# phi's positive part moved from GpSimd to ScalarE, with a new order of all steps, in an fp32 attention and two-MLP kernel on one core

## The chip, the cores and the metric

The kernel runs on one core of a Trainium2 chip. A core has a matrix engine (TensorE, in the profile PE, with PEld for its weight loads), VectorE (DVE), ScalarE (ACT), GpSimd (POOL) and SyncE (SP), which here only issues DMAs. Each engine takes its instructions strictly in the order in which the program lists them and waits on semaphores for the others. The metric is the device time of one execution in microseconds (us), as the median of several runs.

## The reference

The input is a batch of 4 with 8 heads, 576 tokens and 64 columns per head, all in fp32. Attention mixes a causal softmax with a memory read through a feature map phi; two MLPs over the 2304 tokens follow.

```python
def phi(x): return np.where(x > 0, x, np.exp(x) - 1.0) + 1.0
local = softmax(causal(q @ k.T / sqrt(D))) @ v
mem   = (phi(q) @ M_prev) / (phi(q) @ z_prev + 1e-6)
x = g * mem + (1 - g) * local                 # g = sigmoid(beta), one per head
h = x @ w_in;  x = (h * tanh(softplus(h))) @ w_out      # 512 -> 2048 -> 512
h = x @ w_in2; out = (h * sigmoid(h)) @ w_out2
```

phi(x) equals exp(min(x, 0)) + max(x, 0), which is the form that the kernel computes.

## The kernel before, in words

**Attention** runs first, in 16 pairs of heads (`pair_steps` lists the steps of one pair, with an engine, an estimated duration and the steps that they depend on; `Attn.steps` holds the instruction of each). For a pair, PE makes the scores in blocks of 128 queries (`s4`, `s3`, `s2`, `s1`, `s0`, L582 and L621). DVE reads each block from PSUM, adds the mask and takes the row maximum (`r..`, L575). ACT makes the exponentials with their row sums (`e..`, L602). PE transposes the probabilities (`X1`, `X2`, `X3`, `W`, L483), DVE and ACT copy them out of PSUM (L476, L473), and PE multiplies by v and the memory matrix (`Vhi`, `Vlo`, L679). DVE scales the result into `xT` (L683).

**phi** is a side chain of each pair on tile `nq` (128 x 576): `phn` = min(q, 0), `phe` = its exponential on ACT (L503), `phu` = max(q, 0), `phf` = their sum (L505), all but `phe` on POOL. Then POOL multiplies by z_prev (`phz` L506, `phy` L509), DVE adds up and inverts (`phr` L510, `phg` L511, `phd` L513, `phq` L514), and POOL scales phi by the result into the tiles that PE transposes together with the probabilities (`phmh`, `phml` L528, `phm0` L533). POOL also spreads the softmax's divisors (`zg` L631, `n00` L634), which DVE makes (`za` L628, `zd` L630). Tiles `e` and `u` have two buffers each.

**The MLPs** follow on the same core, each product split into seven fp32r products of halves (L985 to L987 for the first matrix, L1053 for the second). Their weights are decoded on ACT and DVE (L789, L799, L801, L803, L806) and the first ones also combined on POOL (L832, L851, L854); eight of these weight tiles are decoded while attention runs or just after it. The first input operands are split by ACT and DVE (L956, L949) from `xT`.

**The order.** `Steps.plan` builds one order of all steps of the whole program before any instruction is issued: at each moment it gives each free engine, out of the steps whose inputs and buffers are there by the estimated durations, the one with the earliest due time. The due times are moved by a table, `SHIFT`, one number for each kind of step. So durations in `pair_steps` and the numbers in `SHIFT` decide where each instruction stands in each engine's queue, attention and MLPs alike. `gate` steps turn beta into g: a load on SP, an exponential on ACT (L431) and ten small operations on DVE (L434 to L449).

Of the kernel before, what the change touches and what calls it, by code (L numbers as in the profile page):

```python
# [202 lines left out]
P = 128  # L203
# [3 lines left out]
ST = 64  # L207
# [9 lines left out]
def mm(n, k=1):  # L217
    return k * max(0.109, n / 2215)
# [40 lines left out]
def pair_steps():  # L259
# [4 lines left out]
    E("phn", "G", 0.75, ["ldnq"])  # L264
    E("phe", "A", 0.58, ["phn"])
    E("phu", "G", 0.75, ["ldnq"])
    E("phf", "G", 1.25, ["phe", "phu"])
    E("phz", "G", 1.25, ["phf"])
    E("phy", "G", 0.36, ["phf"])
# [8 lines left out]
    for i in (4, 3, 2, 1):  # L278
        for x in range(2 if i == 4 else 1):
            n = SA if i == 4 else width(i)  # L280
            E(f"s4{x}" if i == 4 else f"s{i}", "P", mm(n, 4) + 0.07, qk)
# [14 lines left out]
        if i == 1:  # L296
            m.group("s", ("s0", "P", 0.25, qk), [("r00", "D", dve(ST), ["s0"], 0.17)])
            E("e00", "A", act(ST, False, 2), ["r00"])
            m.uses.append(("sm", "r00", ["r00"], ["e00"]))
            exps = ["e00"] + [f"e{x}{y}" for x in range(1, 5) for y in range(2)]  # L300
            E("za", "D", 0.15, exps)
            E("zd", "D", 0.15, ["za"], 0.1)
            E("zg", "G", 1.0, ["zd"])
            E("phq", "D", 0.12, ["za", "phd"])
            E("phmh", "G", 0.75, ["phq"])
            E("phml", "G", 0.75, ["phq"])
            E("phm0", "G", 0.36, ["phd"])
            E("n00", "G", 0.43, ["zd"])
            evict("W", 0.52, ["phmh", "phml"] + exps[1:], 512)
            m.twin("t", ("RT", "P", 0.30, ["zg"]), [[("RTAh", "A", act(256), ["RT"])], [("RTBh", "A", act(256), ["RT"])]])  # L310
# [5 lines left out]
        if i == 2:  # L316
            hi = [f"e{x}{j}" for x in (3, 4) for j in range(2)]
            evict("X1", 0.52, hi, 512)
            evict("X2", 0.42, hi, 384)
            V("hi", (1, 2))  # L320
        if i == 1:
            lo = [f"e{x}{j}" for x in (1, 2) for j in range(2)]
            evict("X3", 0.48, lo + ["n00", "phm0"], 384, 0.14)
            V("lo", (3,))
# [12 lines left out]
class Attn:  # L337
# [153 lines left out]
    def steps(self, p):  # L491
# [10 lines left out]
        f["phn"] = lambda: nc.gpsimd.tensor_scalar(self.get(p, "e"), s["nq"], 0.0, None, op0=ALU.min)  # L502
        f["phe"] = lambda: nc.scalar.activation(s["e"], s["e"], AF.Exp)  # L503
        f["phu"] = lambda: nc.gpsimd.tensor_scalar(self.get(p, "u"), s["nq"], 0.0, None, op0=ALU.max)
# [406 lines left out]
class Moe:  # L911
# [522 lines left out]
```

## Time and profile before

| | us |
|---|---|
| median of 3 runs (lowest, highest) | 965.44 (965.17, 966.11) |
| the profiled execution | 967.41 |
| its span, first to last instruction | 965.5 |
| attention, from the start to the first matmul of the MLPs | 195.28 |
| from there to the end | 770.2 |

The profiled execution took 1.9 us more than its span, and 2.0 us more than the median of the other runs. Lines "Lnnn" are lines of the kernel above. A group of instructions is written as line, engine, operation, output tile <- input tiles, and its busy time. The granted clock is a share of TensorE's full clock.

### The profile page before, as it was taken

How to read it: one execution, taken by the hardware profiler on the slowest of the kernel's cores; microseconds unless marked ns; L12 is line 12 of the kernel's file. 1: busy time of each engine (PE TensorE's matmuls, PEld its weight loads, DVE VectorE, ACT ScalarE, POOL GpSimd, SP SyncE). 2: the span in 40 equal slices, each digit the busy share in tenths (PEclk: the TensorE clock that was granted, in tenths of full speed). 3: DMA queues.
4: the chain of work that ended last, by engine and by line, in shares of the span. 5: the costliest groups of instructions: out<-in, count | busy, mean ns of one | idle time of the engine just before them, and what ended most of it. 6: DMA issues, size and time to landing. Idle time of an engine off the chain costs nothing.

```text
span 965.5 us, 17322 instructions
## 1 busy us (share of the span) xinstructions
PE 932.6 (97%) x6656; PEld 821.3 (85%) x6656; DVE 673.1 (70%) x1541; ACT 496.3 (51%) x1167; POOL 171.1 (18%) x191
## 2 busy tenths in 40 slices
PE   6998989889999999999999999999999999999998
PEld 4665656679999999999999999999898998989986
DVE  6898889896577668773858798947656756654333
ACT  5787888875655334442533564654533433434330
POOL 7989999600000000000000000000000000000000
PEclk9898999999999999999999999999999999999999
DMA  6443542256536811660176435623650275023512
GB/s 217 123 161 109 167 163 89 73 212 264 229 107 207 275 66 54 218 224 23 51 249 214 190 158 178 249 92 94 207 219 1 71 264 183 1 78 128 183 55 98
DMA packets 57218, 143.47 MB, mean 149 GB/s; under 512 B 6960, under 2 KB 24368, under 8 KB 57136
## 3 DMA queue, kind: packets, MB, share of 16 engines
q1 hardware_dynamic: 56992, 142.04, 42.8%
q8 instruction: 52, 0.85, 0.4%
q10 hardware_dynamic: 144, 0.33, 0.1%
q14 instruction: 30, 0.25, 0.1%
HBM read 104.60 MB, written 37.75 MB: 147 GB/s over the span
## 4 chain that ended last, share of the span: by engine, by line
PE 82%; POOL 6%; ACT 5%; DVE 4%; issue 1%; DMA 1%; SPq 0%; POOLq 0%; ACTq 0%
PE acc L1053 42%; PE psX L985 7%; PE psX L986 7%; PE psX L987 7%; PE psY L986 3%; PE psY L987 3%; PE psY L985 3%; PE ps_t L679 2%; PE psW L987 2%; PE psW L986 2%; PE psW L985 2%; PE ps_s L582 2%; PE ps_t L483 1%; POOL e L502 1%; ACT Ph L602 1%
## 5 line engine op out<-in xcount | busy, mean ns | idle before, releaser
L1053 PE MATMUL acc<-g,w 128*128 128x320 f32 (+1 forms) x1152 | 218.1, 337 | 0.0
L1053 PE MATMUL acc<-w,g 128*128 128x512 f32 x864 | 215.3, 394 | 0.0
L1053 PEld LDWEIGHTS acc<-g,w 128*128 128x128 f32 x1152 | 184.0, 188 | 13.3
L1053 PEld LDWEIGHTS acc<-w,g 128*128 128x128 f32 x864 | 157.5, 188 | 30.1
L1016 ACT COPY vt<-psX 128x256 f32<-128x256 f32 (+1 forms) x192 | 75.4, 397 | 134.3 <-PE psX L987 122.8
L1074 DVE TENSOR_TENSOR xT<-acc,xT 128x512 f32<-128x512 f32 (+1 forms) x126 | 77.2, 613 | 84.4 <-PE acc L1053 83.7
L1026 DVE TENSOR_TENSOR g<-vt,g 128x512 fp32r<-128x512 f32 (+1 forms) x128 | 94.9, 754 | 40.3 <-ACT g L1025 39.4
L1014 DVE TENSOR_TENSOR vt<-psY,vt 128x256 f32<-128x256 f32 (+1 forms) x128 | 58.0, 457 | 92.6 <-ACT vt L1016 46.1
L1025 ACT CAST g<-vt 128x512 fp32r<-128x512 f32 (+1 forms) x128 | 83.5, 672 | 36.8 <-PE acc L1053 35.7
L985 PE MATMUL psX<-x,w 128*128 128x320 f32 (+1 forms) x256 | 75.8, 296 | 0.0
L986 PE MATMUL psX<-x,w 128*128 128x320 f32 (+1 forms) x256 | 75.7, 296 | 0.0
L987 PE MATMUL psX<-x,w 128*128 128x320 f32 (+1 forms) x256 | 75.6, 295 | 0.0
L582 PE MATMUL ps_s<-kT,qT 64*128 64x288 f32 (+3 forms) x320 | 69.2, 487 | 6.2 <-DMA kT<-in_kT_dram 4.7
L1022 ACT ACTIVATE vt<-vt 128x640 f32<-128x640 f32 (+1 forms) x64 | 43.7, 685 | 47.2 <-DVE vt L1014 46.9
L1020 ACT ACTIVATE vt<-vt 128x256 f32<-128x256 f32 (+1 forms) x64 | 28.3, 444 | 74.8 <-DVE vt L1014 74.8
L575 DVE CUSTOM_DVE_ANT_0 sm<-ps_s,mask 128x320 f32<-128x320 f32 (+3 forms) x128 | 56.6, 472 | 8.9 <-PE ps_s L582 7.2
L1021 ACT ACTIVATE vt<-psX 128x256 f32<-128x256 f32 (+1 forms) x64 | 26.0, 407 | 50.2 <-PE psX L987 50.1
L1014 DVE TENSOR_TENSOR vt<-psW,vt 128x256 f32<-128x256 f32 (+1 forms) x64 | 29.1, 455 | 31.1 <-PE psW L987 29.2
L985 PEld LDWEIGHTS psX<-x,w 128*128 128x128 f32 x256 | 48.2, 188 | 1.8 <-issue 0.2
L986 PEld LDWEIGHTS psX<-x,w 128*128 128x128 f32 x256 | 48.3, 189 | 1.6
L602 ACT ACTIVATE Ph<-sm,m 128x576 f32<-128x576 f32 (+1 forms) x64 | 45.7, 720 | 6.1 <-DVE m L575 5.8
L987 PEld LDWEIGHTS psX<-x,w 128*128 128x128 f32 x256 | 48.2, 188 | 0.0
(125 smaller groups left out, 2067.6 us busy)
## 6 DMA issues: line engine op xcount, KB each, us to landing
stg<-in_moe_w_in_dram SPq DMA_DIRECT2D x32, 512.0 KB, 5.0
stg<-in_moe_w_out_dram SPq DMA_DIRECT2D x32, 512.0 KB, 4.0
x<-sp SPq DMA_DIRECT2D x18, 640.0 KB, 5.2
x<-sp SPq DMA_DIRECT2D x18, 512.0 KB, 4.0
sp<-x SPq DMA_DIRECT2D x12, 640.0 KB, 3.1
sp<-x SPq DMA_DIRECT2D x12, 512.0 KB, 4.1
nv<-in_v_dram SPq DMA_DIRECT2D x16, 320.0 KB, 3.0
x1T<-sp01T SPq DMA_DIRECT2D x8, 640.0 KB, 4.4
```

Of the source, the lines that this page charges most:

```text
L575: nc.vector.tensor_tensor_reduce(out, ps, mask, -0.125, init, ALU.add, ALU.min, acc)
L582: nc.tensor.matmul(ps, lhsT=s["qT"][R[j], qcols(i)], rhs=s["kT"][R[j], k0 + cols.start:k0 + cols.stop], start=True, stop=True)
L602: nc.scalar.activation(ptile(i)[:, o:o + w] if i else G("P0")[:, 2], s[f"sm{i}{j}"], AF.Exp, bias=s[f"m{i}"][:, j:j + 1], scale=-1.0, accu ...
L985: nc.tensor.matmul(o, lhsT=W(0, kc), rhs=X(0, kc), start=(n in (1, 2, 7) and kc == 0), stop=False, skip_group_check=True)
L986: nc.tensor.matmul(o, lhsT=W(0, kc), rhs=X(1, kc), start=False, stop=False, skip_group_check=True)
L987: nc.tensor.matmul(o, lhsT=W(1, kc), rhs=X(0, kc), start=False, stop=(kc == 1), skip_group_check=True)
L1014: nc.vector.tensor_tensor(o, self.bank[q, to], o, op=ALU.add)
L1016: f[f"s{n}"] = lambda n=n: nc.scalar.copy(val(*at[n]), self.bank[q, "X"])
L1025: f[f"h{c}"] = lambda c=c: nc.scalar.copy(hi(c), val(c))
L1026: f[f"l{c}"] = lambda c=c: nc.vector.tensor_tensor(self.gt(q, c)[:, 1, :2 * tb], val(c), hi(c).bitcast(F32), op=ALU.subtract)
L1053: nc.tensor.matmul(y, lhsT=a, rhs=b, start=(c == 0 and k == 0), stop=(c == 1 and k == 5))
L1074: nc.vector.tensor_tensor(part, acc, part, op=ALU.add)
```

## The change

max(q, 0) is now a Relu activation on ACT (`phu`), and min(q, 0) is made on POOL as q minus that (`phn`, a TENSOR_TENSOR instead of a TENSOR_SCALAR). So `phn` depends on `phu`, where before both depended on the load alone. Estimated durations of some fifteen steps are altered, and all of `SHIFT`.

```diff
-    E("phn", "G", 0.75, ["ldnq"])
+    E("phu", "A", 0.58, ["ldnq"])
+    E("phn", "G", 1.37, ["phu"])
     E("phe", "A", 0.58, ["phn"])
-    E("phu", "G", 0.75, ["ldnq"])
-    E("phf", "G", 1.25, ["phe", "phu"])
+    E("phf", "G", 1.37, ["phe", "phu"])
     E("phz", "G", 1.25, ["phf"])
-    E("phy", "G", 0.36, ["phf"])
+    E("phy", "G", 0.29, ["phf"])
...
-            E("za", "D", 0.15, exps)
+            E("za", "D", 0.1, exps)
...
-            E("phmh", "G", 0.75, ["phq"])
-            E("phml", "G", 0.75, ["phq"])
-            E("phm0", "G", 0.36, ["phd"])
+            E("phmh", "G", 0.58, ["phq"])
+            E("phml", "G", 0.58, ["phq"])
+            E("phm0", "G", 0.26, ["phd"])
...
-        f["phn"] = lambda: nc.gpsimd.tensor_scalar(self.get(p, "e"), s["nq"], 0.0, None, op0=ALU.min)
+        f["phn"] = lambda: nc.gpsimd.tensor_tensor(self.get(p, "e"), s["nq"], s["u"], op=ALU.subtract)
         f["phe"] = lambda: nc.scalar.activation(s["e"], s["e"], AF.Exp)
-        f["phu"] = lambda: nc.gpsimd.tensor_scalar(self.get(p, "u"), s["nq"], 0.0, None, op0=ALU.max)
+        f["phu"] = lambda: nc.scalar.activation(self.get(p, "u"), s["nq"], AF.Relu)
...
-    ('a', 'ldkT'): -4.8, ('a', 'ldqT'): -0.1, ('a', 'ldnq'): 2.62, ('a', 'ldnv'): 720.14, ('a', 'phn'): -463.56,
+    ('a', 'ldkT'): -8.04, ('a', 'ldqT'): 1.13, ('a', 'ldnq'): 1.53, ('a', 'ldnv'): 829.25, ('a', 'phu'): 231.88,
```

The order shows at three places what moved. First POOL in steady attention, about one pair long; `P_..` is the tile that `phm0` and `n00` write. Before:

```order
L502 TENSOR_SCALAR e<-nq 128x576
L504 TENSOR_SCALAR u<-nq 128x576 x2
L533 TENSOR_TENSOR P_278<-e,c 128x64
L505 TENSOR_TENSOR e<-e,u 128x576
L506 TENSOR_TENSOR u<-e,z 128x512
L509 TENSOR_TENSOR u<-e,y 128x64
L634 TENSOR_SCALAR P_278<-P_278,r,g1s 128x2x64
L631 TENSOR_TENSOR rx<-r,g_102 128x512
L528 TENSOR_TENSOR Pl<-e,c 128x2x128
L528 TENSOR_TENSOR Ph<-e,c 128x2x128
```

And POOL in the changed kernel, about one pair long:

```order
L502 TENSOR_TENSOR e<-nq,u 128x576
L509 TENSOR_TENSOR u<-e,y 128x64
L505 TENSOR_TENSOR e<-e,u 128x576
L506 TENSOR_TENSOR u<-e,z 128x512
L533 TENSOR_TENSOR P_424<-e,c 128x64
L509 TENSOR_TENSOR u<-e,y 128x64
L528 TENSOR_TENSOR Pl<-e,c 128x2x128
L634 TENSOR_SCALAR P_424<-P_424,r,g1s 128x2x64
L631 TENSOR_TENSOR rx<-r,g_102 128x512
L528 TENSOR_TENSOR Ph<-e,c 128x2x128
```

The L504 rows are gone; where one of them often stood between L502 and L505 of a pair there is now a short row or none.

Second the start, on DVE; `ISA` with `sm` is a score reduction of r.., and `bt` and `g` are the gate's tiles. Before:

```order
L405 MEMSET warm 128x1
L575 ISA sm,m_135<-ps_s,mask 128x288
...
L575 ISA sm,m_159<-ps_s,smask 128x64
L575 ISA m_159 128x1
L434 TENSOR_SCALAR bt_100<-bt_100 128x8
L435 RECIPROCAL g<-bt_100 128x8
```

And DVE at the start of the changed kernel:

```order
L405 MEMSET warm 128x1
L434 TENSOR_SCALAR bt_100<-bt_100 128x8
...
L449 COPY bt_105<-bt_100 64x4 x2
L575 ISA sm,m_152<-ps_s,mask 128x288
L575 ISA m_152 128x1
```

The whole gate chain now stands ahead of the first five reductions (four of 288 columns and one of 64), which stood ahead of it. On SP, the first q loads changed places too. Before:

```order
L458 DMA qT<-in_qT_dram 128x576
L458 DMA nq<-in_q_dram 128x576
L462 DMA z<-in_z_prev_dram 128x512
L467 DMA y<-in_z_prev_dram 64x4x64 x2
L428 DMA bt_100<-in_beta_dram 128x8
```

And SP's first rows in the changed kernel:

```order
L458 DMA nq<-in_q_dram 128x576
L462 DMA z<-in_z_prev_dram 128x512
L467 DMA y<-in_z_prev_dram 64x4x64 x2
L458 DMA qT<-in_qT_dram 128x576
L428 DMA bt_100<-in_beta_dram 128x8
```

qT, which the first score needs, went from first place to behind the loads of nq, z and y; beta kept its place.

Third DVE where attention ends and the first splits of the MLPs' input (L949) begin; `val` and `stg` belong to a weight tile's decoding. Before:

```order
L803 SCALAR_TENSOR_TENSOR val<-stg,val 128x512
L791 TENSOR_SCALAR val<-stg 128x512
L806 SCALAR_TENSOR_TENSOR val<-stg,val 128x512
L949 TENSOR_TENSOR x_3523<-xT,x_3523 128x512
L949 TENSOR_TENSOR x_3525<-xT,x_3525 128x512
L949 TENSOR_TENSOR xT<-xT 128x2x256
L683 TENSOR_TENSOR xT<-ps_t,R 128x256
L949 TENSOR_TENSOR xT<-xT 128x2x256
```

And DVE in the changed kernel, a few rows behind its first split:

```order
L949 TENSOR_TENSOR xT<-xT 128x2x256
L799 TENSOR_SCALAR val<-val 128x512
L683 TENSOR_TENSOR xT<-ps_t,R 128x256
L949 TENSOR_TENSOR x0T_3453<-xT,x0T_3453 128x512
L949 TENSOR_TENSOR xT<-xT 128x2x256
L801 TENSOR_SCALAR val<-val 128x512
L949 TENSOR_TENSOR x_3602<-xT,x_3602 128x640
L949 TENSOR_TENSOR x_3601<-xT,x_3601 128x640
```

Two of the first eight weight tiles (four rows each: L799, L801, L803, L806) stand behind the first split in the changed kernel; before, all eight stood ahead of it. On PE the last pair's `Vhi` now stands behind the first three products of the MLPs, where before all of attention stood ahead of them.

## Rows read from the trace of the kernel before

**Rows 1.** The page's first part: busy us, share of the span, instructions.
```profile
PE 932.6 (97%) x6656; PEld 821.3 (85%) x6656; DVE 673.1 (70%) x1541; ACT 496.3 (51%) x1167; POOL 171.1 (18%) x191
```

**Rows 2.** Windows, by stage: length; busy us of each engine; granted clock; DMA.
```profile
0.00:20.00 20.00, 11.61 (x72) 8.64 (x72) 12.58 (x48) 9.85 (x29) 14.29 (x21) 1.00 0.59 202
...
20.00:181.30 161.30, 145.93 (x1711) 98.48 (x1710) 143.65 (x509) 134.38 (x416) 150.87 (x164) 0.94 0.41 131
...
195.28:215.00 19.72, 16.18 (x115) 14.84 (x114) 18.51 (x31) 14.78 (x30) 0.98 (x1) 1.00 0.62 245
215.00:940.00 725.00, 725.00 (x4503) 673.64 (x4502) 478.12 (x912) 324.24 (x661) 0.00 (x0) 1.00 0.44 151
```

**Rows 3.** Waits of PE and DVE from 20 to 200 us: total, times, longest.
```profile
PE ps_t L483 <- POOL Pl L528: 2.3, 3, 1.4
PE ps_t L483 <- POOL Ph L528: 1.9, 3, 1.0
...
DVE c L510 <- POOL u L509: 4.2, 5, 1.2
```

**Rows 4.** One of these waits in the timeline: start, length, engine, operation.
```profile
138.05 0.34 PE L483 MATMUL ps_t<-ident,Pl 64*128 64x64 f32 x4 [1.41 <-POOL Pl L528]
```

**Rows 5.** Windows of 5 us round the last fall of the clock.
```profile
135.00:140.00 5.00, 2.91 (x44) 1.87 (x40) 4.64 (x13) 3.06 (x12) 5.00 (x8) 1.00 0.72 251
140.00:145.00 5.00, 3.94 (x42) 2.58 (x42) 3.74 (x16) 3.08 (x9) 4.20 (x4) 0.58 0.35 107
```

**Rows 6.** Groups of POOL: operation, count, busy us, mean ns, idle before and releaser.
```profile
L502 POOL TENSOR_SCALAR e<-nq 128x576 f32<-128x576 f32 x16 | 26.7, 1671 | 2.5 <-DMA nq<-in_q_dram 2.2
L504 POOL TENSOR_SCALAR u<-nq 128x576 f32<-128x576 f32 x16 | 26.4, 1650 | 0.0
L505 POOL TENSOR_TENSOR e<-e,u 128x576 f32<-128x576 f32 x16 | 23.1, 1446 | 5.1 <-ACT e L503 4.1 <-DVE c L513 0.8
```

**Rows 7.** Group of ACT: the exponential of phi.
```profile
L503 ACT ACTIVATE e<-e 128x576 f32<-128x576 f32 x16 | 11.1, 691 | 3.6 <-POOL e L502 3.5
```

**Rows 8.** Groups of three small DVE operations, to 180 us.
```profile
L628 DVE TENSOR_SCALAR z<-z 128x9 f32<-128x9 f32 x15 | 8.5, 564 | 1.7 <-ACT Pl L602 1.7
...
L514 DVE TENSOR_TENSOR c<-c,z 128x8 f32<-128x8 f32 x15 | 7.0, 468 | 0.2
L511 DVE SCALAR_TENSOR_TENSOR c<-c,bt 128x9 f32<-128x9 f32 x15 | 6.9, 457 | 0.0
```

**Rows 9.** The source line of L628: ns least, median, most.
```profile
L628 DVE TENSOR_SCALAR z<-z x16: 161/318/1402, 19.4 to 184.7; 128x9 f32<-128x9 f32 x16
```

**Rows 10.** Timeline at two places: a pass of POOL, the DVE operation beside it.
```profile
154.33 1.42 POOL L505 TENSOR_TENSOR e<-e,u 128x576 f32<-128x576 f32 x1
...
154.38 1.40 DVE L628 TENSOR_SCALAR z<-z 128x9 f32<-128x9 f32 x1
...
168.02 1.64 POOL L504 TENSOR_SCALAR u<-nq 128x576 f32<-128x576 f32 x1
...
168.23 0.47 DVE L514 TENSOR_TENSOR c<-c,z 128x8 f32<-128x8 f32 x1
```

**Rows 11.** Timeline of the start: SP's queue and DVE.
```profile
2.11 1.40 SPq L467 DMA_DIRECT2D y<-in_z_prev_dram  x2
...
6.16 0.46 DVE L575 CUSTOM_DVE_ANT_0 sm<-ps_s,mask 128x288 f32<-128x288 f32 x1 [5.31 <-PE ps_s L582]
...
7.88 0.22 DVE L575 CUSTOM_DVE_ANT_0 sm<-ps_s,smask 128x64 f32<-128x64 f32 x1
...
9.03 0.17 DVE L434 TENSOR_SCALAR bt<-bt 128x8 f32<-128x8 f32 x1 [0.93 <-ACT bt L431]
...
13.44 0.62 DVE L575 CUSTOM_DVE_ANT_0 sm<-ps_s,mask 128x448 f32<-128x448 f32 x1
```

**Rows 12.** Timeline: two of the four DVE operations of one weight tile.
```profile
190.54 0.41 DVE L801 TENSOR_SCALAR val<-val 128x512 uint32<-128x512 uint32 x1
...
192.07 0.68 DVE L803 SCALAR_TENSOR_TENSOR val<-stg,val 128x512 uint32<-128x512 uint32 x1
```

More of the change, by code (lines that the diff above doesn't have):

```diff
@@ L280, in pair_steps @@
             n = SA if i == 4 else width(i)
-            E(f"s4{x}" if i == 4 else f"s{i}", "P", mm(n, 4) + 0.07, qk)
+            E(f"s4{x}" if i == 4 else f"s{i}", "P", mm(n, 4), qk)
         for j in range(2):
@@ L296, in pair_steps @@
         if i == 1:
-            m.group("s", ("s0", "P", 0.25, qk), [("r00", "D", dve(ST), ["s0"], 0.17)])
+            m.group("s", ("s0", "P", 0.17, qk), [("r00", "D", dve(ST), ["s0"], 0.17)])
             E("e00", "A", act(ST, False, 2), ["r00"])
@@ L304, in pair_steps @@
             E("phq", "D", 0.12, ["za", "phd"])
-            E("phmh", "G", 0.75, ["phq"])
-            E("phml", "G", 0.75, ["phq"])
-            E("phm0", "G", 0.36, ["phd"])
+            E("phmh", "G", 0.58, ["phq"])
+            E("phml", "G", 0.58, ["phq"])
+            E("phm0", "G", 0.26, ["phd"])
             E("n00", "G", 0.43, ["zd"])
-            evict("W", 0.52, ["phmh", "phml"] + exps[1:], 512)
-            m.twin("t", ("RT", "P", 0.30, ["zg"]), [[("RTAh", "A", act(256), ["RT"])], [("RTBh", "A", act(256), ["RT"])]])
+            evict("W", 0.49, ["phmh", "phml"] + exps[1:], 512)
+            m.twin("t", ("RT", "P", 0.25, ["zg"]), [[("RTAh", "A", act(256), ["RT"])], [("RTBh", "A", act(256), ["RT"])]])
         def V(half, groups):
@@ L317, in pair_steps @@
             hi = [f"e{x}{j}" for x in (3, 4) for j in range(2)]
-            evict("X1", 0.52, hi, 512)
-            evict("X2", 0.42, hi, 384)
+            evict("X1", 0.49, hi, 512)
+            evict("X2", 0.37, hi, 384)
             V("hi", (1, 2))
@@ L322, in pair_steps @@
             lo = [f"e{x}{j}" for x in (1, 2) for j in range(2)]
-            evict("X3", 0.48, lo + ["n00", "phm0"], 384, 0.14)
+            evict("X3", 0.44, lo + ["n00", "phm0"], 384, 0.12)
             V("lo", (3,))
```

162 rows, old and new, of the table SHIFT are left out of this document.

## The prediction

> **What bounds the kernel now.** I read the busy shares first, then windows cut by stage, then the waits inside the stage that the change touches.
>
> PE is busy for 932.6 of 965.5 us [rows 1], so the whole looks bound by PE. The windows show that this holds for one stage only [rows 2]: from 215 to 940 us PE never stops (725.00 of 725 us), at full clock. No order of the other engines can gain there; it could only lose. What can be gained lies ahead of that. In steady attention, 20 to 181.3 us, the busiest engine is not PE but POOL: 150.9 of 161.3 us (93.5%), against 145.9 for PE, 143.7 for DVE and 134.4 for ACT. PE is idle for 15.4 us of it, and its mean granted clock is 0.94, which is 0.06 x 161.3 = 9.7 us of full clock that it didn't have.
>
> That POOL sets the pace shows in the waits: PE waits 2.3 + 1.9 us for POOL's `phml` and `phmh`, up to 1.4 us at a time, and DVE waits 4.2 us for `phy` [rows 3]. One of these waits is the one of 1.41 us at 138 us [rows 4]. In that window PE is busy for only 2.91 of 5 us while POOL is busy for all of it, and in the next window the granted clock is at 0.58 [rows 5], that is mostly at the lower of the two levels. So a late POOL costs twice: the wait, and the slow matmuls after it.
>
> **The change part by part.** I sum against the profiled execution, 967.4 us; the median of the runs, 965.4, is 2.0 lower, and I carry this over at the end. Differences within 0.2% (1.9 us) a measurement of this kernel can't tell from none.
>
> *POOL.* Per pair `phu` goes (1.650 us), and `phn` turns from a TENSOR_SCALAR of 1.671 us to a TENSOR_TENSOR. The nearest row is `phf`, of the same shape and also two inputs, 1.446 us [rows 6]. So POOL loses 1.650 + 0.225 = 1.87 us per pair; 14 of the 16 pairs have both passes between 20 and 181.3 us, which makes 26.3 us, and POOL falls to 124.6 us there. It is no longer the busiest.
>
> *ACT.* Relu isn't in the trace. The nearest row is the exponential of the same tile, 0.691 us [rows 7]; a lower bound is 0, an upper one is `phu`'s own 1.65. At 0.69, 14 passes are 9.7 us, and ACT rises to 144.1 us. In the stage that is still below what POOL had.
>
> *The chain of phi.* Before, POOL could run `phu` while ACT ran `phe`. Now POOL waits for `phu`, runs `phn`, and waits for `phe` again with little or nothing in between. POOL already waited 4.1 us for `phe` in all [rows 6]. At up to 0.69 us more on each of 14 passes this is 9.7 us of waiting, which fits into the 161.3 - 124.6 = 36.7 us that POOL now has free. I put 0; if ACT is late by two of its exponentials each time, POOL is full again, which is the case of no gain below.
>
> *DVE beside POOL's passes.* Three small DVE operations per pair (L628, L514, L511, 8 or 9 columns) took 8.5 + 7.0 + 6.9 = 22.4 us for 45 instructions [rows 8], while the fastest of L628 took 0.161 us, the slowest 1.402 [rows 9]. 45 x 0.161 = 7.2, so 15.2 us are waiting, 1.0 us per pair. The timeline shows for what: an L628 that started 0.05 us after a TENSOR_TENSOR of POOL took 1.40 us and ended as that did; an L514 under a TENSOR_SCALAR with 1.43 us left took 0.47 us [rows 10]. So passes with two inputs hold DVE up, those with one input hardly. The change takes away 53.1 us of the second kind and adds 16 x 1.446 = 23.1 us of the first, of which there are at most 171.1 - 53.1 = 118 us now [rows 1, 6]. In proportion the waits grow by a fifth, 0.2 us per pair or 3 us in the stage; 0 if the operations fall elsewhere, and far more if they all meet a long pass (the slower rival).
>
> The Trainium skill's page "SBUF — State Buffer", section "Who interferes with whom", says that VectorE and GpSimd share one pair of ports as an exclusive lock held for a whole instruction, and that the loser fully blocks. Taken for every pass of POOL alike, it would make the waits shrink with POOL's busy time, from 171 to 141 us, a gain of some 2 to 3 us on DVE where I put a loss of 3. For TENSOR_TENSOR this trace agrees; for the TENSOR_SCALAR passes the 0.47 us row doesn't, and I go by the row.
>
> *The start.* The order puts DVE's gate chain ahead of its first five reductions. In the trace these began at 6.16 and ended at 8.1 us, the gate chain waited for beta until 9.03, and the reductions went on at 13.44 [rows 11]. beta's place in SP's queue is the same, so the chain should end at about 13.4 again, and the five reductions come after it: 1.9 us of DVE work that lay in a gap comes onto the path, and ACT's first exponentials wait for it. qT is issued behind nq, z and y, whose issue alone took 1.40 us for y; that is hidden, since the first reduction now waits for beta anyway. I take +2 us, with bounds of 0 (made up for later) and 3 (a Relu of 0.69 stands among the first exponentials too).
>
> *The end of attention.* Two weight tiles' decoding moves from attention to behind it. One tile is two operations of 0.41 and two of 0.68 us [rows 12], so 4.4 us leave DVE's stage and land between 195 and 215 us, where DVE is busy for 18.5 of 19.7 us and PE is idle for 3.5 [rows 2]. Against that PE has the last `Vhi` to fill in with. I take +1, with 0 and 4.4 as bounds.
>
> *The stage.* With all this DVE has 143.7 + 3 - 4.4 = 142.3 us, ACT 144.1, POOL 124.6, and PE 145.9 less what the clock gives back, 136 to 146. If the busiest of the new stage is as full as POOL was (93.5%), 142.3 gives 152.2 us and 146 gives 156.1: 5 to 9 us less. I take 8, near the upper end, because three falls of the clock in the stage go with a late POOL and should become rarer. Sum: -8 + 2 + 1 = -5. So 967.4 - 5 = 962.4 for an execution like the profiled one, and 965.4 - 5 = 960.4 for the median; I write 960.5.
>
> **The rivals.**
>
> *More.* All of the clock comes back (PE 136 us), DVE's waits don't grow (139.3), ACT decides with 144.1, and the stage is 97% full: 148.6 us, 12.7 less; with +2 and 0 this is 954.7. For it speaks that each long stall follows a late POOL; against it that three engines then stand within 8 us of each other.
>
> *No change.* POOL was full, but what PE got from that was only its own waits: 4.2 us [rows 3]. DVE, ACT and PE wait for each other as before, and phi's longer chain through ACT keeps POOL late at some pairs. -4.2 + 2 + 1 = -1.2: 964.2.
>
> *Slower.* DVE becomes the bound through POOL's two-input passes. If each of the three small operations met half of a 1.446 us pass, it would wait 0.72 us, 2.2 per pair against 1.0, so 1.2 x 14 = 16.8 us more: DVE 143.7 - 4.4 + 16.8 = 156.1, at 93.5% a stage of 167 us, 5.7 more; with the start and the end 974. It decides from where the stage exceeds 158.3 us, that is DVE above 148 us: 8.7 us more than 139.3, or 0.6 us more per pair. For it speaks that POOL's passes are now nearly all of this kind; against it that POOL is free for 37 us of the stage.
>
> **How the numbers follow.** Forecast 0.53 (957 to 963.5), more 0.16, no change 0.14, slower 0.17. Faster by over 0.2% is the first two, 0.69; same 0.14; slower 0.17. Half of "more" lies below 953 and two thirds of "slower" above 968.5, 0.08 + 0.11; so the range is 953 to 968.5, and the likeliest case alone has 957 to 963.5.
>
> **What would show it.** Right: POOL's busy time at about 141 us; L502 near 1.45 and L504 on ACT near 0.69; no wait of PE over 1 us for L528; a mean clock above 0.94 in attention; DVE's first reduction at about 13.4 us; the first matmul of the MLPs 5 to 6 us earlier than 195.3; 725 us without a gap behind it. Wrong: L628, L514 and L511 with a mean well above 0.5 us (slower), or PE's idle time unchanged with ACT or DVE as the releaser where POOL was (no change).

## The result and the profile after

| | us |
|---|---|
| the changed kernel, median of 4 runs (lowest, highest) | 952.79 (951.46, 954.36) |
| the kernel before beside it, median of 4 runs | 965.31 (964.67, 966.11) |
| ratio, 95% interval | 0.9871 (0.9853 to 0.9888) |
| the profiled execution after, its span | 952.63, 950.8 |
| first matmul of the MLPs (L985) | 181.24 |
| from there to the end | 769.6 |

12.5 us faster, where 5 were forecast, and 0.2 us below the range. Between the two profiled executions the span fell by 14.7 us; 2 us of that is the profiled execution of before, which lay that much above its median.

The page of the changed kernel, first part, answers to [rows 1].

```profile
PE 922.8 (97%) x6656; PEld 814.5 (86%) x6656; DVE 675.0 (71%) x1541; ACT 504.5 (53%) x1183; POOL 141.0 (15%) x175
```

POOL lost 30.1 us, ACT gained 8.2, DVE 1.9. PE's busy time fell by 9.8 us with the same 6656 matmuls, in line with the granted clock over the whole span (0.999, before 0.988). PE's idle time in the span fell from 32.9 to 28.0 us.

The windows of the changed kernel by stage follow, to be read beside [rows 2]. The second one is cut at 168.5 us for a reason: by then DVE has run as much of attention as it had by 181.3 us before (27 of L683 and 15 of L510 in both, the other kinds to within two), and only the eight operations of the two weight tiles that moved are missing.

```profile
0.00:20.00 20.00, 8.90 (x52) 6.33 (x54) 9.70 (x39) 8.38 (x22) 8.47 (x17) 1.00 0.50 162
20.00:168.50 148.50, 139.61 (x1729) 94.12 (x1727) 142.58 (x509) 142.11 (x436) 122.87 (x147) 1.00 0.46 144
168.50:181.24 12.74, 10.72 (x158) 7.56 (x154) 11.77 (x33) 9.63 (x29) 5.58 (x9) 1.00 0.24 69
181.24:215.00 33.76, 32.25 (x219) 29.52 (x218) 30.94 (x52) 26.79 (x53) 4.08 (x3) 1.00 0.69 273
215.00:940.00 725.00, 725.00 (x4482) 672.13 (x4481) 477.81 (x909) 317.60 (x648) 0.00 (x0) 1.00 0.44 148
```

So DVE stood at this point of attention 12.8 us earlier. All that follows took 784.2 us before (965.5 - 181.3) and 782.3 after (950.8 - 168.5), the two tiles now in it: 1.9 us. These two make the 14.7. The 12.8 us hold the later start too: in the first 20 us DVE did 2.9 us less work than before (9.70 for 12.58), and five score reductions fell into the stage from there; with the eight operations that left it, this is why it has 509 instructions in both. In the stage DVE is busy for 96.0% of the time and ACT for 95.7%, where the fullest engine before, POOL, had 93.5%. POOL stands at 82.7%. The granted clock is 1.00, where it was 0.94, and PE did 18 more matmuls in 6.3 us less of busy time.

The waits of the changed kernel from 20 to 200 us (total, times, longest), answering to [rows 3]:

```profile
POOL e L505 <- ACT e L503: 13.7, 8, 2.8
...
PE ps_t L483 <- DVE xT L683: 1.7, 6, 0.5
...
PE ps_t L483 <- POOL Ph L528: 0.9, 2, 0.8
...
PE ps_t L483 <- POOL rx L631: 0.7, 2, 0.4
...
PE ps_t L483 <- POOL P L634: 0.6, 1, 0.6
```

PE's wait for `phmh` and `phml` is down from 4.2 to 0.9 us, and its wait for POOL in all to 2.2 us, none of it over 0.8; DVE's wait for POOL's `u` (4.2 us) has no row any more. POOL now waits for ACT instead.

The groups of the changed kernel that answer to [rows 6 to 8]:

```profile
L505 POOL TENSOR_TENSOR e<-e,u 128x576 f32<-128x576 f32 x16 | 22.9, 1432 | 17.0 <-ACT e L503 17.0
L502 POOL TENSOR_TENSOR e<-nq,u 128x576 f32<-128x576 f32 x16 | 22.6, 1414 | 5.7 <-ACT u L504 5.6
L504 ACT ACTIVATE u<-nq 128x576 f32<-128x576 f32 x16 | 11.0, 690 | 1.7 <-DMA nq<-in_q_dram 1.7
L628 DVE TENSOR_SCALAR z<-z 128x9 f32<-128x9 f32 x16 | 8.4, 522 | 1.2 <-ACT Pl L602 0.9 <-ACT Ph L602 0.3
L511 DVE SCALAR_TENSOR_TENSOR c<-c,bt 128x9 f32<-128x9 f32 x16 | 8.1, 507 | 0.1
L514 DVE TENSOR_TENSOR c<-c,z 128x8 f32<-128x8 f32 x16 | 5.8, 365 | 0.3
```

The new operations cost what was forecast (1.414 and 0.690 us). The three small DVE operations together hardly moved: 22.3 us for all 48, against 22.8 before (the 22.4 us of [rows 8] are those of 45 of them).

The timeline of the start of the changed kernel answers to [rows 11].

```profile
1.64 1.39 SPq L467 DMA_DIRECT2D y<-in_z_prev_dram  x2
3.07 0.60 SPq L458 DMA_DIRECT2D qT<-in_qT_dram  x1
...
8.72 0.17 DVE L434 TENSOR_SCALAR bt<-bt 128x8 f32<-128x8 f32 x1 [7.86 <-ACT bt L431]
12.87 0.46 DVE L575 CUSTOM_DVE_ANT_0 sm<-ps_s,mask 128x288 f32<-128x288 f32 x1
...
16.11 0.62 DVE L575 CUSTOM_DVE_ANT_0 sm<-ps_s,mask 128x448 f32<-128x448 f32 x1 [1.37 <-PE ps_s L582]
```

DVE waits 7.86 us for the gate chain with nothing done; the first reduction of 448 columns, at 13.44 us before, starts 2.7 us later.

### The profile page after: what moved, and what is told of

Same layout as the page of the kernel before. It is cut to its first block, busy times and chain, and to the rows that moved or that the text cites. A ratio compares the mean times of both kernels' runs of the same rounds, so it can differ in the third digit from the quotient of the medians.

```text
span 950.8 us, 17401 instructions
## 1 busy us (share of the span) xinstructions
PE 922.8 (97%) x6656; PEld 814.5 (86%) x6656; DVE 675.0 (71%) x1541; ACT 504.5 (53%) x1183; POOL 141.0 (15%) x175
## 4 chain that ended last, share of the span: by engine, by line
PE 83%; DVE 7%; ACT 5%; issue 2%; POOL 1%; DMA 0%; SPq 0%; DVEq 0%; POOLq 0%; ACTq 0%
PE acc L1053 42%; PE psX L985 7%; PE psX L986 7%; PE psX L987 7%; PE psY L986 4%; PE psY L987 4%; PE psY L985 4%; DVE sm L575 3%; PE psW L986 2%; PE psW L987 2%; PE psW L985 2%; ACT Pl L602 2%; PE ps_t L483 1%; PE ps_t L679 1%; PE ps_s L582 1%
## 5 line engine op out<-in xcount | busy, mean ns | idle before, releaser
L1053 PEld LDWEIGHTS acc<-g,w 128*128 128x128 f32 x1152 | 184.4, 188 | 13.7
L985 PE MATMUL psX<-x,w 128*128 128x320 f32 (+1 forms) x256 | 75.6, 295 | 0.0
L582 PE MATMUL ps_s<-kT,qT 64*128 64x288 f32 (+3 forms) x320 | 65.8, 466 | 9.0 <-DMA qT<-in_qT_dram 7.3
L575 DVE CUSTOM_DVE_ANT_0 sm<-ps_s,mask 128x288 f32<-128x288 f32 (+3 forms) x128 | 56.8, 472 | 3.1 <-PE ps_s L582 1.7
L986 PEld LDWEIGHTS psX<-x,w 128*128 128x128 f32 x256 | 48.3, 189 | 1.5
L985 PEld LDWEIGHTS psX<-x,w 128*128 128x128 f32 x256 | 48.2, 188 | 1.5
L860 ACT CAST w<-val 128x512 fp32r<-128x512 f32 (+1 forms) x64 | 35.0, 567 | 25.4 <-DVE val L851 13.0
```

Of the source, the lines that this page charges most:

```text
L575: nc.vector.tensor_tensor_reduce(out, ps, mask, -0.125, init, ALU.add, ALU.min, acc)
L582: nc.tensor.matmul(ps, lhsT=s["qT"][R[j], qcols(i)], rhs=s["kT"][R[j], k0 + cols.start:k0 + cols.stop], start=True, stop=True)
L985: nc.tensor.matmul(o, lhsT=W(0, kc), rhs=X(0, kc), start=(n in (1, 2, 7) and kc == 0), stop=False, skip_group_check=True)
L986: nc.tensor.matmul(o, lhsT=W(0, kc), rhs=X(1, kc), start=False, stop=False, skip_group_check=True)
L1053: nc.tensor.matmul(y, lhsT=a, rhs=b, start=(c == 0 and k == 0), stop=(c == 1 and k == 5))
```

## The experiments

Each was timed on one chip beside the kernel before, whose medians there were 965.3 to 966.4 us. Two theories came first: the operations carry the gain, or the new order does.

**The operations alone** (`ops_only`): the kernel before with its own table and its durations, but with the new operations.

```diff
-    E("phn", "G", 0.75, ["ldnq"])
+    E("phu", "A", 0.58, ["ldnq"])
+    E("phn", "G", 1.37, ["phu"])
-    E("phu", "G", 0.75, ["ldnq"])
...
-        f["phn"] = lambda: nc.gpsimd.tensor_scalar(self.get(p, "e"), s["nq"], 0.0, None, op0=ALU.min)
+        f["phn"] = lambda: nc.gpsimd.tensor_tensor(self.get(p, "e"), s["nq"], s["u"], op=ALU.subtract)
-        f["phu"] = lambda: nc.gpsimd.tensor_scalar(self.get(p, "u"), s["nq"], 0.0, None, op0=ALU.max)
+        f["phu"] = lambda: nc.scalar.activation(self.get(p, "u"), s["nq"], AF.Relu)
```

> The new operations alone (Relu on ACT, q minus it on POOL) with SHIFT and all other durations of the kernel before. Theory A, that POOL's load set the pace: POOL falls to 141 us busy, the mean clock in attention rises from 0.94 towards 1, and most of the 12.5 us is here already, 953 to 958 us. Theory B, that the order sought with truer durations made the gain: 962 to 970 us, since the old table was sought for other steps.

Measured: 972.53 us, ratio 1.0071 (1.0055 to 1.0088): slower. Where it lost is in the windows of `ops_only` round the end of attention:

```profile
181.00:196.62 15.62, 14.13 (x163) 9.24 (x159) 13.97 (x33) 9.99 (x31) 5.06 (x7) 0.89 0.35 124
196.62:205.00 8.38, 5.45 (x33) 4.55 (x31) 7.23 (x12) 7.84 (x14) 0.00 (x0) 0.84 0.47 187
205.00:215.00 10.00, 9.82 (x61) 9.62 (x62) 10.00 (x18) 7.22 (x17) 0.00 (x0) 0.80 0.64 258
```

Steady attention, from 20 to 180 us, in `ops_only`:

```profile
20.00:180.00 160.00, 146.20 (x1726) 98.81 (x1725) 150.95 (x519) 143.64 (x436) 128.45 (x151) 0.97 0.44 140
```

and in the kernel before:

```profile
20.00:180.00 160.00, 144.63 (x1701) 97.62 (x1700) 142.51 (x505) 133.08 (x411) 149.66 (x162) 0.94 0.41 132
```

In steady attention the operations alone did help: DVE was busy for 150.95 us in place of 142.51, the clock was 0.97 in place of 0.94, and POOL's last L509 began at 174.5 us, 6.4 earlier than before (180.9). But the first matmul of the MLPs came at 196.62 us, 1.3 later than before. Behind it PE was idle for 3.1 us up to 215 us, no more than the 3.5 of before [rows 2], but from 181 to 215 us the granted clock was 0.80 to 0.89, where before had 1.00. What POOL had given was lost at the end of attention; that the order wasn't fitted to the new operations there is a reading that no run tests.

**The order alone** (`order_only`): the changed kernel with both old operations back on POOL, in the order that was planned for the new ones.

```diff
-        f["phn"] = lambda: nc.gpsimd.tensor_tensor(self.get(p, "e"), s["nq"], s["u"], op=ALU.subtract)
+        f["phn"] = lambda: nc.gpsimd.tensor_scalar(self.get(p, "e"), s["nq"], 0.0, None, op0=ALU.min)
-        f["phu"] = lambda: nc.scalar.activation(self.get(p, "u"), s["nq"], AF.Relu)
+        f["phu"] = lambda: nc.gpsimd.tensor_scalar(self.get(p, "u"), s["nq"], 0.0, None, op0=ALU.max)
```

> The changed kernel's order with the old operations in it: max and min of q both as TENSOR_SCALAR on POOL, max at the place in the order where the Relu stood. Theory A: POOL is at 171 us again and full in attention, PE waits for it, the clock falls: 962 us or more. Theory B: the order keeps at least half of the gain, 959 us or less.

Measured: 970.25 us, ratio 1.0046 (1.0029 to 1.0062): slower. PE's waits from 20 to 180 us in `order_only` are POOL's again, and longer than in [rows 3]:

```profile
PE ps_t L483 <- POOL Pl L528: 3.6, 4, 1.3
PE ps_t L483 <- POOL Ph L528: 3.2, 7, 1.4
```

So each half alone costs time, and together they gain 12.5 us. Neither theory stands by itself.

**One input in place of two** (`phn_one_input`): the changed kernel with `phn` as before, min(q, 0) by TENSOR_SCALAR.

```diff
-        f["phn"] = lambda: nc.gpsimd.tensor_tensor(self.get(p, "e"), s["nq"], s["u"], op=ALU.subtract)
+        f["phn"] = lambda: nc.gpsimd.tensor_scalar(self.get(p, "e"), s["nq"], 0.0, None, op0=ALU.min)
```

> The changed kernel, but min(q, 0) as a TENSOR_SCALAR of q (one input, about 1.65 us) in place of q minus the Relu (two inputs, 1.41 us). If POOL's passes with two inputs hold up DVE and DVE is now the bound, the three small DVE operations fall from a mean of 0.46 us to about 0.37 and the time by 1 to 4 us. If which pass it is doesn't matter, it stays within 1 us, or rises by up to 2 since POOL's chain is 0.24 us longer per pair.

Measured: 953.21 us, ratio 0.9873 (0.9858 to 0.9888), as the changed kernel. L502 takes 1.647 us again, and the three small DVE operations 22.8 us for 48 (changed: 22.3). The kind of this one pass moved neither the time nor this sum by more than 0.5 us.

**The start** (`start_swapped`, later once more as `start_swapped_again` beside `changed_again`, and `start_gate_only`, which has the first move alone): the planned order of the changed kernel with two steps moved.

```diff
-        for k in self.plan():
+        order = self.plan()
+        def move(k, after):
+            order.remove(k)
+            order.insert(order.index(after) + 1, k)
+        move(("gate", "sig"), (0, "r00"))
+        order.remove((0, "ldqT"))
+        order.insert(order.index((0, "ldnq")), (0, "ldqT"))
+        for k in order:
```

> The changed kernel with two moves at the start alone: the gate chain on DVE behind the first five score reductions, and the first load of qT ahead of that of nq; every other step in its place. If the start cost 2 us as forecast, the first matmul of the MLPs comes about 2 us earlier and the time is 950 to 951.5 us. If the delay is made up later, within 1 us of the changed kernel.

> The changed kernel with the gate chain of DVE put behind its first five reductions, qT's load left behind nq, z and y. If the gate chain's place alone costs the forecast 2 us: 2 us less than changed_again. If qT's late load holds the reductions just as long: within 0.7 us of changed_again.

> start_swapped once more (gate chain behind the reductions and qT's load ahead of nq), beside changed_again. The forecast of the start says 2 us less than changed_again; the first run of it pointed to 1.2.

> The changed kernel as it is, for the three others. All theories: 951.5 to 954.4 us.

Measured: `start_swapped` 951.57 us, ratio 0.9854 (0.984 to 0.9869), and again 951.69, 0.9855 (0.984 to 0.9869); `start_gate_only` 952.01, 0.9855 (0.9842 to 0.9869); `changed_again` 953.27, 0.987 (0.9857 to 0.9884). The first 20 us of `start_swapped_again`:

```profile
0.00:20.00 20.00, 10.78 (x62) 8.15 (x64) 12.48 (x44) 10.10 (x26) 8.49 (x18) 1.00 0.55 188
```

and of `changed_again`:

```profile
0.00:20.00 20.00, 8.40 (x49) 5.81 (x50) 9.22 (x37) 7.89 (x20) 8.24 (x17) 1.00 0.46 159
```

The moves bring 3.3 us of DVE work back into the first 20 us, but the time falls by 1.2 to 1.6 us (the same sign in three comparisons, but with intervals that overlap, so the size is uncertain). With the gate chain's place alone it falls by 1.3. Part of a late start is made up later. `start_swapped` has the lowest median of the versions with the whole computation.

**A pass of POOL added** (`pool_pass_added` behind L509, `pool_pass_in_wait` ahead of L505, where it reads a constant tile): does POOL's freed time have a worth?

```diff
+            nc.gpsimd.tensor_tensor(s["u"][:, 8], s["e"][:, 8], self.bt[b]["y"][:, hp], op=ALU.mult)
+            nc.gpsimd.tensor_scalar(self.scratch, s["e"], 0.0, None, op0=ALU.max)
```

> The changed kernel with one more TENSOR_SCALAR pass of 128x576 on POOL per pair, behind L509, into a tile that nobody reads: 1.65 us x 16, of which some 25 us before the end of attention, so POOL stands at about 153 of 161 us there, as full as before the change. If POOL's freed time is the gain, most of it goes: 960 to 967 us, with PE waiting 2 us or more in all for L528 again. If POOL's time had no worth and only the order's other changes count: 952 to 955 us.

> The changed kernel with the added TENSOR_SCALAR pass of pool_pass_added (here of a constant tile) ahead of L505 instead of behind L509: POOL stands there idle for 17.0 us in 9 of the 16 pairs, waiting for ACT's exponential. If a pass costs by its length wherever it stands: 963 to 967 us, as pool_pass_added (965.45). If it costs where it makes phi's chain later: some 12 of its 26 us lie in those waits, and about half of the 12.7 us is lost: 957 to 961.

Measured: 965.45 us, ratio 0.9997 (0.9987 to 1.0008), and 964.74, 0.9981 (0.9972 to 0.999). The first gives the whole gain back, the second all but 1.6 us of it (966.35 for the kernel before beside it). 20 to 180 us in the changed kernel:

```profile
20.00:180.00 160.00, 149.09 (x1873) 101.01 (x1871) 153.47 (x539) 150.50 (x461) 128.45 (x155) 1.00 0.44 139
```

in `pool_pass_added`:

```profile
20.00:180.00 160.00, 144.84 (x1728) 98.59 (x1728) 144.28 (x509) 143.88 (x436) 145.20 (x160) 0.97 0.43 134
```

and in `pool_pass_in_wait`:

```profile
20.00:180.00 160.00, 145.56 (x1747) 98.03 (x1744) 143.02 (x514) 143.98 (x438) 146.12 (x163) 0.97 0.43 134
```

With POOL at 91% DVE and ACT reach 89 to 90%; with POOL at 80% DVE reaches 95.9 and ACT 94.1. The place decided little: ahead of L505 the pass fell into POOL's waits for `phe` (13.7 us from 20 to 180 before it, 3.8 with it, in 20 to 185), and cost 11.5 us (beside `changed_again`) where the other cost 12.7. PE then waited 4.1 us for `rx` and 2.0 for `P`, which POOL makes behind phi. One thing these runs leave open: the planner doesn't know of the added pass, so its plan is about 1.65 us per pair short on POOL, as that of before was. They show what the pass costs in this order, not what it would cost in one planned for it.

**One engine made lighter** each time, in the changed kernel: POOL without `phz`, ACT without the relu (L505 then adds `e` to itself, and L502 takes min(q, 0) as in `phn_one_input`, with which it is compared), DVE's sum L510 over 8 of 64 columns.

```diff
-        f["phz"] = lambda: nc.gpsimd.tensor_tensor(
+        f["phz"] = None
...
-        f["phu"] = lambda: nc.scalar.activation(self.get(p, "u"), s["nq"], AF.Relu)
+        f["phu"] = None
...
-        f["phr"] = lambda: nc.vector.tensor_reduce(out=self.get(p, "c"), in_=s["u"], axis=AX.X, op=ALU.add)
+        f["phr"] = lambda: nc.vector.tensor_reduce(out=self.get(p, "c"), in_=s["u"][:, :, :8], axis=AX.X, op=ALU.add)
```

> The changed kernel without POOL's product L506 (1.27 us x 16), the sum L510 then reads the relu. POOL falls from 128 to about 111 us before the MLPs. If POOL's time has no more worth once it is below the other engines: 951 to 954. If each us of POOL still counts through phi's chain, as it did in pool_pass_added (12.2 us for 25): 944 to 948.

> The changed kernel without its relu on ACT: L502 takes min(q, 0) from q itself as in phn_one_input, L505 adds e to itself. 14 x 0.69 = 9.7 us less on ACT before the MLPs (151.7 to 142), and phi's chain is shorter by one step. Compared with phn_one_input (953.2). If ACT, 94% full, sets the pace of attention now: 944 to 948. If DVE does, as the fuller of the two: 950 to 954.

> The changed kernel with the sum L510 of DVE over 8 of its 64 columns, so 0.735 us becomes some 0.2 and DVE has about 7.5 us less before the MLPs (154.4 to 147). If DVE sets the pace of attention: 945 to 949. If ACT does: 950 to 954.

Measured: `phz_left_out` 947.9 us, ratio 0.9812 (0.9797 to 0.9827); `relu_left_out` 950.19, 0.9834 (0.9815 to 0.9852); `reduce_shortened` 951.36, 0.9849 (0.9833 to 0.9866). Against 952.8 (953.2 for the second) that is 4.9, 3.0 and 1.4 us for about 16 x 1.27, 0.69 and 0.52 us taken away. Per us taken away that is 0.24 on POOL, 0.27 on ACT and 0.17 on DVE. The intervals of these times reach about 1.5 us each way, so the order of the three isn't shown, and the 1.4 us of DVE can't be told from none; that no engine gives back near the whole of what is taken away is clear. By the recorded expectations `relu_left_out` points to DVE as the one that sets the pace, `reduce_shortened` to ACT, and `phz_left_out` to POOL as still counting: no single engine sets it. Part of `phz_left_out` shows on DVE; its groups of the small operations follow, whose line numbers are 2 less than in the changed kernel:

```profile
L626 DVE TENSOR_SCALAR z<-z 128x9 f32<-128x9 f32 x16 | 6.0, 378 | 1.1 <-ACT Pl L600 0.9 <-ACT Ph L600 0.2
L509 DVE SCALAR_TENSOR_TENSOR c<-c,bt 128x9 f32<-128x9 f32 x16 | 5.9, 370 | 0.1
L512 DVE TENSOR_TENSOR c<-c,z 128x8 f32<-128x8 f32 x16 | 3.9, 245 | 0.3
```

22.3 us became 15.8, without a change to these operations. So the 4.9 us aren't POOL's time alone: DVE got 6.5 us lighter with it, and phi's chain shorter.

**The plan.** Six runs give the planner other tables and durations. In `table_empty_...` SHIFT is empty; `table_before` is the changed kernel with the table of before; `table_new_old_operations` has the old operations, planned at 1.61 us each, with the new table and the new durations.

```diff
-SHIFT = {
...
+SHIFT = {}
...
-    E("phu", "A", 0.58, ["ldnq"])
-    E("phn", "G", 1.37, ["phu"])
+    E("phn", "G", 1.61, ["ldnq"])
+    E("phu", "G", 1.61, ["ldnq"])
```

> The kernel before with its table SHIFT empty, so that the planner's own rules alone set the order, with the old operations and their durations. It is the base for the next run. Both theories expect a time well above the kernel before, between 975 and 1020 us, as nothing was sought.

> The changed kernel (new operations, new durations) with SHIFT empty, against table_empty_old. Theory C (the operations make room, and any order that is planned with them can use it; an order that was sought for other operations can't): 5 to 15 us below table_empty_old. Rival D (the operations are worth nothing, the gain is that of a table sought once more): within 3 us of table_empty_old.

> The changed kernel (new operations, new durations) with the table of the kernel before. Theory C: slower than the kernel before or no faster, 963 to 975 us, since the table was sought for other operations and durations. Rival E (the durations taken from the trace carry the gain, the table little of it): 951 to 958 us.

> The new operations with an empty table as in table_empty_new (978.05), but with the durations of all other steps as in the kernel before. If the operations alone make the 18 us between the two empty tables: 976 to 981. If the durations taken from the trace make them: 990 to 997.

> The old operations (both passes on POOL, planned at 1.61 us each) with the new durations of all other steps and an empty table, against table_empty_new (978.05) and table_empty_old (996.22). If the operations make the difference: 990 to 997. If a plan with true durations does, whatever the operations: 978 to 984.

> The old operations, planned at 1.61 us each, with the new durations and the new table. order_only had the same operations and table in an order that was planned for a relu on ACT (970.25). Theory C (a table is worth its full gain only with the operations that it was sought with, and the old operations leave POOL full): 966 to 980. If the new table and the durations are the better ones for any operations: 953 to 960.

| operations | durations | table | us | ratio (interval) |
|---|---|---|---|---|
| old | before | empty | 996.22 | 1.031 (1.0295 to 1.0326) |
| old | new, 1.61 each | empty | 975.14 | 1.0096 (1.0075 to 1.0118) |
| new | before | empty | 981.24 | 1.0153 (1.0136 to 1.017) |
| new | new | empty | 978.05 | 1.0125 (1.011 to 1.014) |
| new | new | of before | 968.44 | 1.0021 (1.0011 to 1.0031) |
| old | new, 1.61 each | new | 978.95 | 1.0141 (1.0119 to 1.0163) |

In the third row `phu` and `phn` have their new durations, all other steps the old ones. The first and the fourth row seemed to give the operations 18 us (theory C); the second took that away. The plan of before has `phn` and `phu` at 0.75 us each, while they take 1.67 and 1.65 [rows 6]; 1.61 in their place, with the other new durations, makes the untuned order 21 us better, and then the old operations are even 2.9 us ahead of the new (the intervals just overlap). So in this untuned order the operations are worth nothing, or less. A table pays most with the operations that it was sought with: the new one is worth 25.3 us with the new operations (978.05 to 952.79), and costs 3.8 with the old (975.14 to 978.95); that of before is worth 30.8 us with the old operations and durations (996.22 to 965.4), and 9.6 with the new (978.05 to 968.44).

The windows of `table_empty_old_true_durations` show how full the old operations can keep POOL:

```profile
20.00:180.00 160.00, 144.65 (x1680) 101.02 (x1679) 142.56 (x494) 132.09 (x405) 152.03 (x161) 0.96 0.42 137
```

It is 95.0%, at a clock of 0.96. POOL's 150.87 us of work in the stage [rows 2] would at that share take 158.8 us, at the 96.0% that DVE reaches now 157.2, at 100% 150.9, where the new operations took 148.5. By this estimate, which takes POOL as the only limit, a better order for the old operations could have had 2.5 to 4.1 us of the 12.8, at the very most 10.4; the rest needs the lighter POOL. No order was sought for the old operations at their true durations, so how much of it they could really have had stays open.

A light POOL isn't enough for full engines either, as `table_empty_new` shows:

```profile
20.00:180.00 160.00, 145.79 (x1627) 100.84 (x1626) 138.04 (x479) 136.92 (x408) 119.01 (x139) 0.91 0.44 138
```

With POOL at 74.4% DVE stands at 86.3% and ACT at 85.6% there.

## Why the prediction was wrong

*What bounds.* Right for the end: 725.00 of 725 us of PE behind 215, before and after. Half right for attention: POOL was the fullest, and a pass added to it takes the gain back (`pool_pass_added`), but it did not set the pace alone: POOL and ACT each give something back when made lighter, POOL at 82.7% too. And not all three falls of the clock went with a late POOL. Two did (PE waited 1.03 us for `phmh` at 77.7 us, and 1.41 at 138); before the first, at about 35 us, PE had waited 1.0 us for DVE's `xT` and 0.2 for POOL.

*POOL and ACT.* Right: 1.88 us less per pair (30.1 / 16) for the forecast 1.87, L504 0.690 for 0.69, and in the stage 122.9 and 142.1 us for 124.6 and 144.1.

*The chain of phi*, put at 0. In the stage POOL waits 13.7 us for `phe` (2.7 before) and none for `phu`, 11.0 more, near the 9.7 of the working; the other 3.3 us for `phe` and the 5.6 for `phu` lie in the first 20 us. It fits into POOL's free time, as forecast. Not free, though: without the relu, so with a shorter chain and a lighter ACT, 3.0 us come back. `relu_left_out` doesn't separate the two.

*DVE beside POOL's passes*, put at +3. It was 0 (22.8 to 22.3 us for all 48). The reading of [rows 10] holds in the timelines of all 48 operations. Before, 17 of them began with over 0.35 us of a two-input pass of POOL left, and all 17 lasted to its end (within 0.15 us); 12 began so under a one-input pass, and one did. In the changed kernel it is 24 of 25 under two-input passes. Runs agree: `phz_left_out` takes 20.3 us of two-input passes away, and 6.5 us of waiting; the added one-input passes moved the sum by +1.8 (behind L509) and -1.6 us (ahead of L505). But the size in proportion didn't hold: 31 in place of 22 began under a two-input pass, but with less of it left (0.63 us in the mean, before 0.75), and 16 in place of 11 met no pass at all. Whether `phn` meets these operations hangs on its place (`phn_one_input`).

The page "SBUF — State Buffer" of the Trainium skill, section "Who interferes with whom", states that VectorE and GpSimd contend for one shared port pair, which is an exclusive lock. Taken for every pass alike, 2 to 3 us should have gone, as POOL was busy 30 us less; the sum fell by 0.5. And 26.9 us of added one-input passes should have cost as much as the 20.3 us of `phz` gave back, 6.5, but cost 1.8 and -1.6. For the two-input passes the trace agrees with the page, for the one-input passes it doesn't.

*The start*, +2: right in place and sign, and about two thirds of its size (1.2 to 1.6). *The end of attention*, +1: it was -0.6 (first matmul of the MLPs to the end: 770.2 before, 769.6 after); PE's idle time between that matmul and 215 us went from 3.5 to 1.5 us.

*The stage*, -8 (5 to 9): this is the step that failed, with -12.8, and that with the cost of the start in it, which the sum had beside it; without, it is about -14. Its work came out within 0.3 us (DVE 142.6 for 142.3), in part by luck: the 3 us of waits did not come, and 2.9 us of work fell in from the first 20 us. What failed is "the busiest of the new stage as full as POOL was (93.5%)". DVE was 96.0% and ACT 95.7% full, PE ran at a clock of 1.00 in place of 0.94, and so 142.6 us took 148.5 and not 152.2 to 156.1. How full the busiest can be isn't a constant that one engine hands to the next: in this order DVE and ACT stop at 89 to 90% with POOL at 91%, and reach 94 to 96% with POOL at 80%; in an untuned order they stay at 86% with POOL at 74% (`table_empty_new`). The conditions of the rival "more" (all of the clock back, DVE's waits unchanged, 97% full) nearly came: a clock of 1.00, the small operations' sum unchanged, 96.0%; and 952.8 is 1.9 below its 954.7.

What the working left out is the plan. It took POOL's load and the durations apart from the order. The diff and [rows 6] together show that the old plan was 1.82 us per pair short on these two passes of POOL (1.50 for 3.32), while the new has 0.58 and 1.37 for 0.69 and 1.41. In the untuned order true durations were worth 21 us (996.22 to 975.14); what the error cost the tuned order of before, no run shows. The rival "slower" did not come; nor did POOL's lateness through ACT ("no change").

## What to carry to other kernels

When a load is taken off the fullest of several nearly full engines, don't give the next one the old one's fullness: the others can fill up further, and the clock can come back with it, as here, so work out the gain for the share that the next engine can reach at best as well. Where a table or a search sets the order, operations and order are one change: test each half with the other half undone, and compare the planned durations with the trace before anything else. To learn which engine counts, add or take away a pass on each in turn, and look at what else it moves: the busy shares alone didn't tell it here.

## What the runs showed of the hardware

On POOL a pass with one input is not the cheaper one: min(q, 0) of 128x576 fp32 by TENSOR_SCALAR took 1.647 us (`phn_one_input`), the TENSOR_TENSOR of the same shape 1.414 us. An 8- or 9-column operation on DVE that began under a two-input pass of POOL lasted to the end of that pass (17 of 17 before, 24 of 25 in the changed kernel, of those with over 0.35 us of it left), one under a one-input pass in 1 of 12 cases (before). Taking POOL's 16 two-input products away made three small DVE operations, which don't touch them, 6.5 us shorter in all (22.3 to 15.8), while 16 added one-input passes lengthened them by 1.8 us at one place (24.1) and shortened them at the other (20.7).
